# Projections, gated scan, silu and z in blocks of three chunks instead of segments of two, each in a PSUM bank of its own, with a new instruction list

**Chip, cores, metric.** One core of one Trainium2 chip. Times are device microseconds (us) of one execution; "span" is the time from the first to the last instruction of the profiled execution, which is 1.7 us or so shorter. Engines: TensorE (PE, its weight loads PEld), VectorE (DVE), ScalarE (ACT), GpSimd (POOL), SyncE (SP). The "granted clock" is the share of full speed that TensorE's clock was given. Every instruction is issued from one helper, so all have one line (L98, L99 or L100) in the profiles. Lower is better.

## The reference, cut to what matters

```python
# attention: B=4, H=8, S=768, D=48
for t in range(S):
    cur = einsum('bhd,bhe->bhde', u * k[t], v[t])
    y[t] = einsum('bhd,bhde->bhe', r[t], state + cur)
    state = w[t][..., None] * state + einsum('bhd,bhe->bhde', k[t], v[t])
x = y, heads side by side                     # (4, 768, 384)
proj = x @ w_in                               # 384 -> 2 * 512: val, gate
h = exp(A_log) * h + val[t]   for every t     # the gated scan over the sequence
out = (silu(gate) * h) @ w_out                # 512 -> 384
```

## The kernel before: the parts that the change and the argument touch

The sequence of 4 x 768 is cut into 24 chunks of 128 steps. A chunk of attention goes through all engines: products r\*P, k\*N (`Q`, `K`), transposes, scores (`sc`), the masked scores (`At`), the state (`S`), the output (`y`), and its transpose `xT`. The second half of the kernel works on segments of two chunks:

```python
SEG = 2 * C                                    # C = 128
xTs = ring("xT", 2, [128, 3, S_], BF16)        # two whole batches
hTs = ring("hT", 2, [128, NG, S_], BF16)
zs  = ring("z", 3, [128, NG, SEG], BF16)       # NG = 4 groups of 128 channels
att = psum.tile([C, 2, HP, C], F32)            # one tile of scores, no second one
mms = [psum.tile([128, 512], F32, name=f"mm{i}") for i in range(3)]

def project(m, g0, at):                        # two groups in one bank
    ps = mms[at].rearrange("p (j t) -> p j t", j=2)
    for j in range(2):
        for kk in range(3):
            pe.matmul(ps[:, j, :], w_in_sb[:, kk, (g0+j)*128:(g0+j+1)*128],
                      T["xT", b][:, kk, s*SEG:(s+1)*SEG], start=(kk==0), stop=(kk==2))
    return ps

def scn(m, gg):                                # VectorE, 256 steps
    dve.tensor_tensor_scan(hT[:, gg, s*SEG:(s+1)*SEG], a_f[...], T["pv", m, gg//2][:, gg%2, :],
                           0.0 if s == 0 else hT[:, gg, s*SEG-1:s*SEG], MUL, ADD)

def sl(m, q):                                  # ScalarE, 2 x 256 elements
    lut("silu", T["z", m][:, 2*q:2*q+2, :], T["pg", m, q], Silu)

def z(m, *, on):                               # VectorE ("d") or GpSimd ("p"), 4 x 256 elements
    MULT[on](T["z", m], T["z", m], T["hT", b][:, :, s*SEG:(s+1)*SEG])

def rk(m):                                     # both inputs in SBUF, always VectorE
    dve.tensor_mul(T["rk", m], T["rk", m], T["k", m])

def At(n):                                     # one input in PSUM (att), frees att for the next sc
    dve.tensor_mul(At_n, T["sc", n], mask)
```

The order of all instructions is a list of words in the program, one word an operation: `z.2:d` is the product z of segment 2 on VectorE, `K.5:p` the k\*N product of segment 5 on GpSimd. Each engine runs its own words strictly in the order of the list (in the timeline of VectorE below, the starts at 100.08, 102.01, 103.51, 105.59 and 106.05 us are the words `z.2.0`, `rk.9`, `z.2.1`, `y.15` and `At.17` of the changed list); semaphores do the rest. A cut of it:

```
... At.10 sl.0.0 cs.7.P:20 lw.4 sl.1.1 z.2:d out.9 ex.7.P.0 yT.8 z.1:d pv.3.1:1 lw.5
z.0:d adv.9 red.5 K.6:p xT.8 ld.9.w ex.7.P.1 tr.11 y.9 ...
```

## Time and profile before

| | before |
|---|---|
| time, median of 3 runs | 150.94 us (149.77 to 150.99) |
| profiled run | 149.59 us, span 147.9, mean granted TensorE clock 0.976 |
| VectorE busy | 123.4 us of the span |
| GpSimd busy | 93.7 us |
| start of y of chunks 8, 13, 18, 23 | 65.07, 92.41, 117.61, 135.70 us |

Read the table from its last row: y of a chunk is the last VectorE step of its attention, so the y starts are a clock of how far the kernel has got. They divide the span in a front (to y of 8), a middle (to y of 23), and a tail. In the middle VectorE is almost never idle (busy 69.63 of 70.63 us).

### The profile page before, as it was taken

How to read it: one execution, taken by the hardware profiler on the slowest of the kernel's cores; microseconds unless marked ns; L12 is line 12 of the kernel's file. 1: busy time of each engine (PE TensorE's matmuls, PEld its weight loads, DVE VectorE, ACT ScalarE, POOL GpSimd, SP SyncE). 2: the span in 40 equal slices, each digit the busy share in tenths (PEclk: the TensorE clock that was granted, in tenths of full speed). 3: DMA queues.
4: the chain of work that ended last, by engine and by line, in shares of the span. 5: the costliest groups of instructions: out<-in, count | busy, mean ns of one | idle time of the engine just before them, and what ended most of it. 6: DMA issues, size and time to landing. Idle time of an engine off the chain costs nothing.

```text
span 147.9 us, 3833 instructions
## 1 busy us (share of the span) xinstructions
PE 119.2 (81%) x1512; PEld 83.1 (56%) x1512; DVE 123.4 (83%) x169; ACT 99.0 (67%) x181; POOL 93.7 (63%) x83
## 2 busy tenths in 40 slices
PE   0286873899698778996199989998798899999990
PEld 0133541585475555775085667876576576777750
DVE  3027997577985799999999999989999999999750
ACT  3285626876746597999177979989677635664561
POOL 7806243194797969649490499999252897928500
PEclk9999999999999999999757999999999999999999
DMA  3999998999999899999999999975998996530435
GB/s 55 236 190 234 195 207 180 239 202 213 231 195 234 160 250 221 196 195 317 149 207 192 168 218 225 145 213 83 180 242 171 218 287 184 144 111 0 160 118 205
DMA packets 101026, 27.98 MB, mean 189 GB/s; under 512 B 95760, under 2 KB 101008, under 8 KB 101008
## 3 DMA queue, kind: packets, MB, share of 16 engines
q1 hardware_dynamic: 101008, 27.73, 94.7%
q8 instruction: 12, 0.20, 0.6%
q14 instruction: 6, 0.05, 0.1%
HBM read 21.43 MB, written 4.72 MB: 177 GB/s over the span
## 4 chain that ended last, share of the span: by engine, by line
DVE 44%; PE 27%; SPq 11%; DMA 6%; issue 6%; ACT 4%; DVEq 0%; ACTq 0%
PE mm L100 15%; DVE hT L100 12%; SPq L100 11%; DVE At L100 8%; DVE rk L100 8%; PE trp L100 5%; PE yk L100 5%; DVE y L100 5%; DVE z L100 4%; DMA w<-in_w_dram 4%; DVE dvec L100 3%; DMA k<-in_k_dram 2%; PE att L100 2%; DVE S L100 2%; ACT QK L100 1%
## 5 line engine op out<-in xcount | busy, mean ns | idle before, releaser
L100 PE MATMUL mm<-xT,w_in_sb 128*128 128x256 bf16 x288 | 39.6, 282 | 0.8 <-ACT xT L100 0.6
L100 PEld LDWEIGHTS <-w_in_sb 128*128 128x128 bf16 x288 | 27.3, 100 | 6.7 <-issue 1.8
L100 POOL TENSOR_TENSOR qk<-k,N 128x768 bf16<-128x768 f32 x11 | 21.8, 1981 | 14.3 <-DMA k<-in_k_dram 14.3
L100 DVE TENSOR_TENSOR At<-att,mask 128x1024 bf16<-128x1024 f32 x24 | 29.0, 1210 | 1.2 <-PE att L100 1.1
L100 POOL TENSOR_TENSOR qk<-r,P 128x768 bf16<-128x768 f32 x10 | 19.6, 1959 | 7.6 <-DMA r<-in_r_dram 7.4
L100 DVE TENSOR_TENSOR_SCAN hT<-a_f,hT,mm 128x256 bf16<-128x256 f32 x32 | 22.3, 730 | 1.3 <-PE mm L100 1.3
L100 POOL TENSOR_TENSOR dv<-v,dvec 128x768 f32<-128x768 f32 x9 | 13.3, 1473 | 14.6 <-DVE dvec L100 11.6
L100 ACT COPY QK<-trp 128x1024 bf16<-128x1024 bf16 x18 | 18.2, 1014 | 5.9 <-PE trp L100 5.7
L100 PEld LDWEIGHTS <-qk 128*48 128x48 bf16 (+1 forms) x304 | 16.0, 114 | 10.8 <-issue 7.6
L100 POOL TENSOR_TENSOR rk<-r,u_b 128x768 f32<-128x768 f32 x9 | 16.7, 1861 | 4.5 <-DMA u_b<-in_u_dram 4.5
L100 PEld LDWEIGHTS <-QK 48*128 48x128 bf16 x352 | 11.4, 103 | 13.4 <-ACT QK L100 5.9
L100 PE MATMUL mm<-w_out_sb,z 128*128 128x384 bf16 x96 | 18.9, 331 | 0.0
L100 DVE TENSOR_TENSOR rk<-rk,k 128x768 f32<-128x768 f32 x12 | 17.6, 1469 | 0.0
L100 ACT COPY osb<-mm 128x384 f32<-128x384 f32 x24 | 11.4, 479 | 8.1 <-PE mm L100 7.7
L100 ACT ACTIVATE z<-mm 128x512 bf16<-128x512 f32 x24 | 13.9, 599 | 3.8 <-PE mm L100 3.5
L100 PE MATMUL trp<-ident,qk 128*128 128x128 bf16 x144 | 15.3, 269 | 1.2 <-ACT xT L100 0.9
L100 ACT COPY xT<-trp 128x384 bf16<-128x384 bf16 x24 | 11.5, 481 | 6.7 <-PE trp L100 6.3
L100 DVE TENSOR_TENSOR y<-yk,dv 128x384 bf16<-128x384 f32 x24 | 13.1, 544 | 3.5 <-PE yk L100 3.4
L100 ACT ACTIVATE N<-mm 128x384 f32<-128x384 f32 x24 | 10.9, 489 | 7.6 <-PE mm L100 7.5
L100 PE MATMUL att<-QK 48*128 48x128 bf16 x192 | 11.2, 247 | 4.6 <-ACT QK L100 3.7
L100 ACT ACTIVATE P<-mm 128x384 f32<-128x384 f32 x24 | 10.8, 494 | 5.0 <-PE mm L100 5.0
L100 ACT ACTIVATE lwp<-w 128x768 bf16<-128x768 f32 (+1 forms) x13 | 10.2, 795 | 6.1 <-DMA w<-in_w_dram 5.9
(52 smaller groups left out, 182.0 us busy)
## 6 DMA issues: line engine op xcount, KB each, us to landing
k<-in_k_dram SPq DMA_DIRECT2D x24, 192.0 KB, 4.6
r<-in_r_dram SPq DMA_DIRECT2D x24, 192.0 KB, 4.8
v<-in_v_dram SPq DMA_DIRECT2D x24, 192.0 KB, 4.7
out_dram<-osb SPq DMA_DIRECT2D x24, 192.0 KB, 2.4
w<-in_w_dram SPq DMA_DIRECT2D x11, 384.0 KB, 5.4
stage<-in_moe_w_in_dram SPq DMA_DIRECT2D x4, 384.0 KB, 4.9
stage<-in_moe_w_out_dram SPq DMA_DIRECT2D x2, 384.0 KB, 4.6
w<-in_w_dram SPq DMA_DIRECT2D x2, 192.0 KB, 3.4
```

The costliest lines, as they stand in the source:

```text
L100: return lambda *args, **kwargs: self.tc.keep_in_program_order(op(*args, **kwargs))
```

## The change

The intent is fewer fixed costs: 384 steps at a time instead of 256 make 32 scans instead of 48 and 192 projection matmuls instead of 288, and a bank that holds one group is free again after one scan. z is cut in halves so that it can be spread over two engines. The list was worked out anew.

```diff
-    xTs = ring("xT", 2, [128, 3, S_], BF16)
-    hTs = ring("hT", 2, [128, NG, S_], BF16)
-    zs = ring("z", 3, [128, NG, SEG], BF16)
+    xTs = ring("xT", 3, [128, 3, BL], BF16)        # BL = 3 * C
+    hTs = ring("hT", 3, [128, NG, BL], BF16)
+    zs = ring("z", 3, [128, NG, BL], BF16)
...
-    def project(m, g0, at):
-        ps = mms[at].rearrange("p (j t) -> p j t", j=2)
-        for j in range(2):
-            for kk in range(3): ...
+    def project(mb, gg, at):
+        ps = mms[at][:, :BL]
+        for kk in range(3):
+            pe.matmul(
+                ps, w_in_sb[:, kk, gg * 128 : (gg + 1) * 128], T["xT", mb][:, kk, :],
+                start=(kk == 0), stop=(kk == 2))
...
+    def scn(mb, gg):
         dve.tensor_tensor_scan(
+            hT[:, gg, :], a_f[:, gg : gg + 1].to_broadcast([128, BL]), T["pv", mb, gg],
+            T["hT", mb - 1][:, gg, BL - 1 : BL] if mb * BL % S_ else 0.0, MUL, ADD)
...
-        MULT[on](T["z", m], T["z", m], T["hT", b][:, :, s * SEG : (s + 1) * SEG])
+        rows = slice(2 * q, 2 * q + 2)
+        MULT[on](T["z", mb][:, rows, :], T["z", mb][:, rows, :], T["hT", mb][:, rows, :])
... (the whole list is new; the place that the result turns on:)
+ sc.17 z.2.0:d sl.2.3 tr.16 ld.10.r.0 rk.9 sl.2.2 out.15 QK.16 pg.3.0:1 z.2.1:d ld.10.k.0
+ pg.4.2:2 y.15 dv.8:p sl.3.0 pg.3.3:0 At.17 sl.4.2 ld.11.w pv.4.0:1 sl.3.3 pg.4.0:2 vc.8:a K.9:p
+ scn.4.0 sc.16 pg.4.3:0 ship.1 sl.4.0 At.16 ... trd.18 out.16 ru.10:p S.17:d ...
```

In the list the words r\*P on VectorE go from 3 to 6, k\*N on VectorE from 2 to 4, r\*u on VectorE from 3 to 4, dv on VectorE from 3 to 2. (A word may be half a product.)

## The prediction

> **What bounds the kernel now.** I read the page's shares first, then busy time by stage, then the chain that ended last, the groups, and last the VectorE (DVE) and SyncE timelines. The shares show no single bound:
>
> ```profile
> PE 119.2 (81%) x1512; PEld 83.1 (56%) x1512; DVE 123.4 (83%) x169; ACT 99.0 (67%) x181; POOL 93.7 (63%) x83
> ...
> DVE 44%; PE 27%; SPq 11%; DMA 6%; issue 6%; ACT 4%; DVEq 0%; ACTq 0%
> ```
>
> VectorE has the most work and the largest part of the chain. The stage table (busy us of PE, PEld, DVE, ACT, POOL with counts, then granted clock, DMA share, GB/s) separates four regimes:
>
> ```profile
> 0.00:9.20 9.20, 2.15 (x13) 0.81 (x14) 1.43 (x10) 4.19 (x9) 6.06 (x33) 1.00 0.92 153
> 9.20:24.00 14.80, 10.51 (x117) 6.22 (x115) 12.73 (x16) 8.07 (x17) 5.11 (x3) 1.00 1.18 202
> 24.00:52.00 28.00, 24.05 (x304) 16.27 (x304) 20.63 (x29) 18.29 (x35) 20.20 (x12) 1.00 1.10 211
> 52.00:65.00 13.00, 11.18 (x159) 8.66 (x155) 12.97 (x16) 12.00 (x21) 8.65 (x5) 1.00 1.12 217
> 65.00:136.00 71.00, 63.08 (x873) 45.70 (x871) 70.00 (x93) 51.03 (x94) 51.24 (x29) 0.95 0.91 184
> 136.00:147.90 11.90, 8.26 (x60) 5.43 (x57) 5.61 (x9) 5.37 (x11) 2.39 (x2) 0.98 0.42 150
> ```
>
> To 9.2 the kernel waits for its first inputs. From 9.2 to 52 VectorE idles 9.4 us, in hand-overs and waits for loads. From 52 to 136 it is busy 83.0 of 84.0 us: it is the bound, and what it gains or loses there moves the end one for one. From 136 TensorE streams the last projections and outputs without a gap and VectorE has time to spare. The rows behind this:
>
> ```profile
> L100 DVE TENSOR_TENSOR At<-att,mask 128x1024 bf16<-128x1024 f32 x24 | 29.0, 1210 | 1.2 <-PE att L100 1.1
> L100 DVE TENSOR_TENSOR_SCAN hT<-a_f,hT,mm 128x256 bf16<-128x256 f32 x32 | 22.3, 730 | 1.3 <-PE mm L100 1.3
> L100 DVE TENSOR_TENSOR rk<-rk,k 128x768 f32<-128x768 f32 x12 | 17.6, 1469 | 0.0
> L100 DVE TENSOR_TENSOR_SCAN hT<-a_f,mm 128x256 bf16<-128x256 f32 x16 | 10.3, 670 | 0.0
> L100 DVE TENSOR_TENSOR z<-z,hT 128x1024 bf16<-128x1024 bf16 x7 | 9.1, 1332 | 0.1
> L100 POOL TENSOR_TENSOR qk<-r,P 128x768 bf16<-128x768 f32 x10 | 19.6, 1959 | 7.6 <-DMA r<-in_r_dram 7.4
> ```
>
> The rk product has minimum 927 ns and mean 1469; z has minimum 679 and mean 1332. That stretching is about 12 us in all (12 x 0.54 for rk, 7 x 0.65 for z, 1.25 for one r*u product). It falls on products with both inputs in SBUF, while GpSimd (POOL) runs one too:
>
> ```profile
> 75.59 2.06 POOL L100 TENSOR_TENSOR qk<-k,N 128x768 bf16<-128x768 f32 x1
> 75.90 2.56 DVE L100 TENSOR_TENSOR rk<-rk,k 128x768 f32<-128x768 f32 x1
> ```
>
> [...] Here 24 projections of 256 columns start in 2.86 us (119 ns each) and 24 output matmuls of 384 in about 4.0 us (167 each)[...].
>
> **The change, part by part.** I use spacing of back-to-back instructions of the VectorE timeline, which is some 70 to 90 ns less than a printed duration, since they overlap: At 1.13 us, y 0.46, S 0.26, rk and dvec 0.86, a scan 0.66 (0.60 where it starts from zero), a 768-wide product 0.87, z 0.62.
>
> 1. *Scans.* 48 of 256 become 32 of 384: equal elements, 16 fixed costs fewer. 32 x 0.66 + 16 x 0.60 = 30.7 us[...]. Saves 2.0 us of VectorE.
> 2. *Projections.* 288 matmuls of 256 columns become 192 of 384: 73,728 columns either way. 48 groups at 0.66 us against 64 at 0.5: 31.7 and 32. TensorE gains nothing but 96 weight loads of 100 ns, which mostly lie beside matmuls. A bank now holds one scan, not two, and comes free sooner after its three matmuls.
> 3. *Silu.* 24 of 512 elements (599 ns; spacing 0.49) become 32 of 384 (0.385, from 0.82 ns an element between the 384- and 512-wide rows): 11.8 to 12.3 us on ScalarE. Switches between exponential and silu tables, counted in both lists, stay at six loads. Nothing on the path.
> 4. *z.* Halves of 768 elements, 10 on VectorE and 6 on GpSimd, for 7 and 5 of 1024: VectorE 10 x 0.487 = 4.9 against 4.3; GpSimd 9.6 against 10.7.
> 5. *Work moved by the new list.* Counted from the lists, VectorE takes three more whole r*P products, two more whole k*N and one more r*u, and gives one dv away: 6 x 0.87 - 0.87 = +4.35 us. GpSimd loses about 9 us by that, some 10 with z.
> 6. VectorE in all, uncontended and without start-up: -2.0 + 0.6 + 4.35 = +2.9 us (108.2 to 111.0 as I sum all words).
>
> Where this falls matters. I summed the work listed ahead of each chunk's y. Up to y of chunk 8 (65.1 us before) both lists give VectorE 41.8 us, GpSimd 30.8 before and 19.0 after, TensorE 36.2 and 33.0, loads 13.2 and 12.4 MB. Most of the moved products are thus in the stage where VectorE idles, and replace a GpSimd product of 1.8 us by one of 0.95 within a dependent loop. From y of 8 to y of 23 VectorE has 61.1 before and 63.3 after. After y of 23 TensorE has 7.4 us before and 8.8 after: the last block is three chunks, so eight groups of projections (4.0 us) follow the last y instead of four (2.6).
>
> **Sum.** Front: idle is some 10 us ahead of 65, and I judge that 3 to 6 go: -4.5. Middle: +2.2 of work, plus contention. Fourteen products with two SBUF inputs lost about 0.55 us each there; the new list has 20, less a little for shorter GpSimd z: +1.5 to 3, taken as +2. Lost bubbles: TensorE once waited 4.1 us for a bank under two scans, and its clock fell to 0.55 and 0.60 in the next eight us (72 to 80); if that does not return, up to -2, taken as -1. I walked the last block by hand: y, 0.33 transposes, 0.48 copy, then eight projections, four scans of 0.93 in turn and seven outputs end about 10.1 us after y of 23, where before it was 8.65: +1.5. Together -4.5 + 2.2 + 2 - 1 + 1.5 = +0.2 us: no gain I can derive. A list that was worked out anew was presumably chosen because its whole schedule came out shorter, which I cannot see in sums; for this I take off 1.5 us.
>
> **Rivals.**
> *A, the schedule is the gain.* The loop in the front tightens fully and start-up idle falls by 8 us: 143 to 147. For: GpSimd falls from 30.8 to 19.0 us by y of 8, single-scan banks, fewer bytes wanted early. Against: TensorE itself is busy 24.05 of 28 us at 24 to 52, so there is little room.
> *B, VectorE becomes a harder bound.* The extra products are stretched as rk is today (1469 against 927), and the longer tail is paid in full: 152 to 155. For: 83.0 of 84.0 us busy. Against: GpSimd is 10 us emptier over the whole run.
> *C, supply sets the pace.* SyncE issues loads from 0.8 to 95 us almost without a gap, and the DMA share is about 1.1 to 65 us:
>
> ```profile
> q1 hardware_dynamic: 101008, 27.73, 94.7%
> ...
> POOL qk L100 <- DMA k<-in_k_dram: 14.3, 6, 4.2
> ```
>
> The change moves the same bytes in as many transfers, so whatever the engines gain ends in waits for k, r or v, and the time stays at 149 to 151. Against: later, SyncE waits 14.0 us for finished outputs, so supply is not short there.
>
> **Range and chances.** The before is 150.94 us by median, 149.59 in the profiled run with a span of 147.9. With -1.3 us net I predict 149.5 us. Front (3 us either way), contention (2), tail (1), and run differences (1) give about 3.9 in quadrature; I take 145.5 to 153.5. Faster by over 2% means below 147.9 (0.30); slower means over 153.96 (0.15); the rest, 0.55, is within.
>
> **What would show each step.** Right: 32 scans near 0.94 and 1.00 us; 192 projections of 384 columns and an unchanged busy TensorE within 3 us; VectorE busy 124 to 128 us, GpSimd 81 to 86; y of chunk 8 at 59 to 63 us; last y to end 13 to 13.5 us against 11.65; six table loads. Wrong: [...]VectorE below 122 us (contention fell with GpSimd's load, and I had the sign wrong); y of chunk 8 no earlier than 65 (supply bound, rival C); a new wait of several us of VectorE in the middle, where I assume none; a tail no longer than before.

## The result, and the profile after

| | before | after |
|---|---|---|
| median | 150.49 us (149.77 to 150.99, 4 runs) | 155.32 us (154.75 to 155.92, 4 runs) |
| ratio of fast runs | | 1.0325 (95%: 1.0251 to 1.0399): slower |
| profiled run | 149.59, span 147.9, clock 0.976 | 155.84, span 154.1, clock 0.956 |
| front, to y of 8 | 65.07 | 60.22 (-4.85) |
| middle, y of 8 to y of 23 | 70.63 | 80.23 (+9.6) |
| tail, from y of 23 | 12.20 | 13.65 (+1.45) |

A ratio here is the mean time of one kernel's fast runs over that of the other's in the same rounds, so not quite the ratio of the medians that are quoted. Executions over 1.5% slower than the fastest of the same kernel are left out of the means. The change lost 3%; the prediction had 149.5 us, with 153.5 as its upper end.

The page of the changed kernel, its shares and the chain of waits that ended last:

```profile
PE 121.0 (78%) x1416; PEld 72.0 (47%) x1416; DVE 129.5 (84%) x161; ACT 100.3 (65%) x189; POOL 84.2 (55%) x79
...
DVE 37%; PE 32%; issue 10%; ACT 6%; DMA 6%; POOL 4%; SPq 3%; DVEq 0%; POOLq 0%; ACTq 0%
```

VectorE has 6.1 us more to do than before. Yet its part of the chain fell from 44 to 37%, and TensorE's grew, and so did "issue", the time in which the engine waited for nothing that the profile shows. The groups of instructions of the changed kernel (total us, then mean ns):

```profile
L99 PE MATMUL mm<-xT,w_in_sb 128*128 128x384 bf16 x192 | 40.8, 346 | 2.0 <-DVE hT L99 1.8
L99 DVE TENSOR_TENSOR_SCAN hT<-a_f,hT,mm 128x384 bf16<-128x384 f32 x16 | 16.0, 1005 | 1.1 <-PE mm L99 0.8
L99 DVE TENSOR_TENSOR rk<-rk,k 128x768 f32<-128x768 f32 x12 | 15.3, 1274 | 0.0
L99 DVE TENSOR_TENSOR_SCAN hT<-a_f,mm 128x384 bf16<-128x384 f32 x16 | 14.8, 939 | 1.0 <-PE mm L99 0.9
L99 DVE TENSOR_TENSOR z<-z,hT 128x768 bf16<-128x768 bf16 x10 | 13.8, 1394 | 0.1
```

The scans cost just what was expected of them (939 and 1005 ns, for 0.94 and 1.00 us). z did not: its ten halves take 1394 ns on the mean, where the shortest took 545 (of the wholes of 1024 elements before: 679), so 8.5 us of their 13.8 is time spent blocked.

"Blocked" and "stretched" stand for what the timelines of before and after show of VectorE's products with two SBUF inputs. Of those with 768 elements of f32 input, 29 began with no GpSimd instruction running, or with at most 0.12 us of one left, and took 0.93 to 0.96 us; 13 began with 0.3 us or more of one left and took 1.11 to 2.56 us; one began at the same time as one (86.46 us, after) and took 0.95. The masked scores, with one input in PSUM, took 1.19 to 1.23 us and the reductions to dvec, with one input, 0.92 to 0.95, beside GpSimd or not.

Busy time by stage, before (stretch, its length, busy us of PE, PEld, DVE, ACT, POOL with counts, granted clock, DMA share, GB/s):

```profile
0.00:65.07 65.07, 47.96 (x584) 31.96 (x584) 47.83 (x69) 42.63 (x78) 40.02 (x53) 1.00 1.10 202
65.07:135.70 70.63, 62.71 (x869) 45.44 (x869) 69.63 (x92) 50.84 (x93) 50.94 (x29) 0.95 0.92 185
135.70:147.90 12.20, 8.56 (x64) 5.69 (x61) 5.91 (x9) 5.50 (x11) 2.69 (x2) 0.98 0.41 146
```

The same three stages after, then four us of the middle at a time:

```profile
0.00:60.22 60.22, 41.61 (x522) 25.50 (x523) 46.97 (x65) 38.89 (x72) 28.32 (x47) 0.97 1.13 203
60.22:140.45 80.23, 69.41 (x839) 41.34 (x838) 75.72 (x90) 55.08 (x105) 51.02 (x29) 0.94 0.89 171
140.45:154.10 13.65, 9.96 (x59) 5.19 (x56) 6.85 (x9) 6.28 (x13) 4.87 (x3) 1.00 0.41 145
104.00:108.00 4.00, 0.81 (x12) 0.55 (x12) 4.00 (x4) 0.79 (x2) 3.33 (x2) 1.00 0.48 111
108.00:112.00 4.00, 4.00 (x46) 2.18 (x46) 2.41 (x4) 2.00 (x4) 0.00 (x0) 0.57 0.01 4
```

In the middle VectorE is busy 75.7 us instead of 69.6 (+6.1) and idle 4.5 us instead of 1.0 (+3.5); that is the +9.6. By place, 4.7 of it comes before y of 13, where the front's lead is used up (92.25 us, and 92.41 before), 5.2 between y of 13 and y of 18, and -0.3 after that. Of the +6.1, 3.3 is stretching: over the unblocked durations the products with two SBUF inputs lose 11.9 us there, and lost 8.6 before.

The two last rows show a hole. From 104 to 108 us TensorE works 0.81 us of four while VectorE is full; from 108 to 112 it is the other way about, the clock is at 0.57, and the DMA moves 4 GB/s. The timeline of VectorE in the changed kernel (start, length) tells what fills it:

```profile
98.94 1.21 DVE L99 TENSOR_TENSOR At<-att,mask 128x1024 bf16<-128x1024 f32 x1
100.08 2.01 DVE L99 TENSOR_TENSOR z<-z,hT 128x768 bf16<-128x768 bf16 x1
102.01 1.57 DVE L99 TENSOR_TENSOR rk<-rk,k 128x768 f32<-128x768 f32 x1
103.51 2.15 DVE L99 TENSOR_TENSOR z<-z,hT 128x768 bf16<-128x768 bf16 x1
105.59 0.54 DVE L99 TENSOR_TENSOR y<-yk,dv 128x384 bf16<-128x384 f32 x1
106.05 1.21 DVE L99 TENSOR_TENSOR At<-att,mask 128x1024 bf16<-128x1024 f32 x1
```

GpSimd in the same stretch:

```profile
99.86 1.82 POOL L99 TENSOR_TENSOR qk<-k,N 128x768 bf16<-128x768 f32 x1
...
102.74 2.51 POOL L99 TENSOR_TENSOR rk<-r,u_b 128x768 f32<-128x768 f32 x1
```

And TensorE, where the bracket is its idle time before the instruction and what ended it:

```profile
101.52 2.60 PE L99 MATMUL mm<-xT,w_in_sb 128*128 128x384 bf16 x15
107.31 0.40 PE L99 MATMUL att<-QK 48*128 48x128 bf16 x8 [3.19 <-DVE At L99]
```

Read the three together. The half products z of block 2 and the product rk of segment 9 stand in VectorE's list ahead of y of 15 and the masked scores of chunk 17. GpSimd's k\*N begins at 99.86 and its r\*u at 102.74, each ahead of a z. Without blocking z, rk, z would take 0.54 + 0.93 + 0.54 = 2.0 us; they take 5.7. TensorE runs out its projections at 104.1 and then cannot score chunk 16, because the one tile of scores is still waiting to be masked. It idles 3.19 us. From 108.2 us, 0.9 us after it has come back, its clock is halved for 3.4 us (0.50 over 108.2 to 111.6). SyncE has a transposing copy (`trd.19`) in its queue, whose buffer is that of chunk 16 and comes free with the output matmuls of chunk 16; it waits 7.2 us for them, to 111.4, with loads and stores queued behind it, so the DMA stops too.

Such a hole is nothing new. VectorE of the kernel before:

```profile
66.67 4.26 DVE L100 TENSOR_TENSOR z<-z,hT 128x1024 bf16<-128x1024 bf16 x3
```

and its TensorE:

```profile
73.48 0.82 PE L100 MATMUL mm<-lwp,triP 64*128 64x384 bf16 x4 [4.01 <-DVE hT L100]
```

Three z in a row took 4.26 us, and TensorE idled 4.0. The prediction saw that hole, and reckoned that the new list would be rid of it.

### The profile page after: what moved, and what is told of

Read it like the earlier page. It is cut to its first block, busy times and chain, and to the rows that moved or that the text cites.

```text
span 154.1 us, 3607 instructions
## 1 busy us (share of the span) xinstructions
PE 121.0 (78%) x1416; PEld 72.0 (47%) x1416; DVE 129.5 (84%) x161; ACT 100.3 (65%) x189; POOL 84.2 (55%) x79
## 4 chain that ended last, share of the span: by engine, by line
DVE 37%; PE 32%; issue 10%; ACT 6%; DMA 6%; POOL 4%; SPq 3%; DVEq 0%; POOLq 0%; ACTq 0%
PE mm L99 19%; DVE hT L99 10%; DVE At L99 7%; DVE z L99 6%; PE trp L99 6%; PE yk L99 5%; DVE y L99 4%; DVE qk L99 4%; DVE rk L99 3%; SPq L99 3%; DMA r<-in_r_dram 3%; DMA v<-in_v_dram 3%; PE att L99 2%; DVE S L99 2%; POOL qk L99 2%
## 5 line engine op out<-in xcount | busy, mean ns | idle before, releaser
L99 PE MATMUL mm<-xT,w_in_sb 128*128 128x384 bf16 x192 | 40.8, 346 | 2.0 <-DVE hT L99 1.8
L99 POOL TENSOR_TENSOR qk<-k,N 128x768 bf16<-128x768 f32 x9 | 17.6, 1952 | 18.2 <-ACT N L99 14.2
L99 PEld LDWEIGHTS <-w_in_sb 128*128 128x128 bf16 x192 | 17.9, 101 | 15.1 <-issue 6.0
L99 ACT ACTIVATE z<-mm 128x384 bf16<-128x384 f32 x32 | 15.2, 491 | 10.4 <-PE mm L99 10.1
L99 POOL TENSOR_TENSOR qk<-r,P 128x768 bf16<-128x768 f32 x7 | 14.9, 2129 | 10.9 <-ACT P L99 10.2
L99 PE MATMUL trp<-ident,qk 128*128 128x128 bf16 x144 | 14.8, 262 | 5.8 <-DVE qk L99 4.5
L99 DVE TENSOR_TENSOR_SCAN hT<-a_f,hT,mm 128x384 bf16<-128x384 f32 x16 | 16.0, 1005 | 1.1 <-PE mm L99 0.8
L99 DVE TENSOR_TENSOR_SCAN hT<-a_f,mm 128x384 bf16<-128x384 f32 x16 | 14.8, 939 | 1.0 <-PE mm L99 0.9
L99 DVE TENSOR_TENSOR rk<-rk,k 128x768 f32<-128x768 f32 x12 | 15.3, 1274 | 0.0
L99 DVE TENSOR_TENSOR y<-yk,dv 128x384 bf16<-128x384 f32 x24 | 13.1, 545 | 2.5 <-PE yk L99 2.3
L99 DVE TENSOR_TENSOR z<-z,hT 128x768 bf16<-128x768 bf16 x10 | 13.8, 1394 | 0.1
L99 PE MATMUL mm<-lwp,triN 64*128 64x384 bf16 (+1 forms) x46 | 8.0, 401 | 7.3 <-ACT lwp L99 5.7
```

What stands on the lines that cost most here:

```text
L99: return lambda *args, **kwargs: self.tc.keep_in_program_order(op(*args, **kwargs))
```

## The experiments

The theory after this reading, the **place theory**: the loss is where the blocked products stand, with the attention loop waiting right behind them, and is worth some 4 to 5 us. Rivals: the **amount theory**, that VectorE was simply given too many products with two SBUF inputs, wherever they stand; later the **supply theory**, that loads set the pace, and the **clock theory**, that the fall of TensorE's clock is the loss. Kernels of one group ran on the same chip. Every edit is to words of the list unless it says otherwise; results are right unless it says otherwise.

**1. The two z moved back behind the masked scores.**

```diff
- sc.17 z.2.0:d ... pg.3.0:1 z.2.1:d ... At.17 ... At.16 ... S.17:d yT.15
+ sc.17 ... pg.3.0:1 ... At.17 ... At.16 ... S.17:d z.2.0:d z.2.1:d yT.15
```

> The two halves of z of block 2 stay on VectorE but move in its list from before the mask products of chunks 17 and 16 to after the state product of chunk 17, where VectorE stood idle 1.5 us. Work per engine is unchanged. Amount theory (the middle is longer because VectorE has more work there): no change, 154.5 to 156. Place theory (the loss is made where stretched products stand ahead of a mask product for which TensorE waits, 3.2 us of TensorE idle and then a clock of 0.57): the products meet an idle GpSimd, 3 us of stretching and the idle go, 150.5 to 152.5. Supply theory (the late stages wait for loads): no change or under 1 us.

Median 150.95 us (150.32 to 152.96) beside 151.47 of before on that chip, ratio 0.998 (0.9918 to 1.0042): the same as before. Against the changed kernel's 155.32, measured in another round, that is 4.4 us from moving two words. VectorE in this kernel:

```profile
109.17 1.01 DVE L98 TENSOR_TENSOR z<-z,hT 128x768 bf16<-128x768 bf16 x2
```

Both halves now take 1.01 us together instead of 2.01 and 2.15, and the hole in TensorE is gone: from y of 14 to y of 18 it is 19.95 us instead of 24.45. That stretch in the changed kernel, and then here:

```profile
98.22:122.67 24.45, 19.17 (x223) 10.86 (x224) 22.83 (x26) 14.66 (x30) 13.11 (x8) 0.93 0.74 137
99.82:119.77 19.95, 17.64 (x223) 10.39 (x224) 19.54 (x25) 14.65 (x30) 12.49 (x8) 1.00 0.87 165
```

Of the 4.5 us, 3.3 are busy time of VectorE (22.83 to 19.54) and 1.2 its idle time (1.62 to 0.41). So this edit changes two things at once: where the z stand, and how long they last, 0.5 us each at the new place. The profiled run (152.96) is 1.6 us behind the changed kernel at y of 13 (93.83 us), so only this later stretch is compared.

**2. The two z on GpSimd, at their old place.**

```diff
- z.2.0:d ... z.2.1:d
+ z.2.0:p ... z.2.1:p
```

> The same two halves go to GpSimd at their old place. VectorE loses 4.2 us of measured time at 100 to 106 us. Amount theory: 151 to 152. Place theory: as the run before, 150.5 to 152.5, if GpSimd's later products (dv of 8, k*N of 9) are not wanted at once; it has 6 us idle at 107 to 113. If GpSimd now stands waiting for silu with the next products behind it: 155 to 158.

153.43 us (150.99 to 155.41), ratio 1.0158 (1.0085 to 1.0231), unclear by the 2% line. In the profiled run, which is the quickest (150.99), the hole is gone: y of 14 to y of 18 takes 21.18 us, and no wait of TensorE in the middle is over 1.6 us. The runs scatter over 4 us, so no more is drawn from it.

**3. Three of the added products given back to GpSimd, the two z left alone.**

```diff
- K.5:d (after Q.5 and ru.6)   Q.7:d   Q.8:d
+ K.5:p (right after Q.5)      Q.7:p   Q.8:p
```

> The three products that the new list moved to VectorE in the middle (k*N of 5, r*P of 7 and 8) go back to GpSimd, k*N of 5 right after r*P of 5. VectorE loses 2.6 us of bare work and 1.7 of stretching. Amount theory: 151 to 152. Place theory: only the first one stood before a wait of TensorE, so 153 to 154.5, and more stretching of what stays on VectorE.

155.78 us (155.12 to 156.31), ratio 1.0312 (1.026 to 1.0363): as slow as the changed kernel. VectorE is still busy 128.5 us: it has fewer products, but, with three more on GpSimd, its rk and z lose more (17.2 us of stretching instead of 15.8). The same hole stands there, from y of 14 at 97.44 to y of 15 at 104.81. **The amount theory falls here.** Taking three products away does nothing while the two z stay in their place, though VectorE's busy time fell by 1.0 us only; experiment 4 takes more.

**4. All z of blocks 0 to 6 on GpSimd.**

```diff
- z.0.0:d z.0.1:d z.1.0:d z.1.1:d z.2.0:d z.2.1:d z.3.0:d z.3.1:d z.5.1:d
+ z.0.0:p z.0.1:p z.1.0:p z.1.1:p z.2.0:p z.2.1:p z.3.0:p z.3.1:p z.5.1:p
```

> All z but those of the last block go to GpSimd at their places in the list: VectorE loses 9 products, 4.4 us bare and 8.5 of stretching; GpSimd gains 14.8 of 29 idle us in the middle. Amount theory: 146 to 149. Place theory: GpSimd now waits in order for scans and silu with the r and k products behind it, and rk meets a busier GpSimd: 151 to 158.

151.84 us (150.09 to 153.44), ratio 1.0014 (0.9937 to 1.0091): as good as experiment 1, with VectorE down to 123.2 us busy and GpSimd up to 99.9. 6.3 us less work on VectorE gives no more than moving two words, which again speaks for place and not for amount. What is left is two other waits of TensorE of 1.9 and 2.0 us, the first for a z that is now on GpSimd.

**5. More moves of the same kind, on top of experiment 1.**

```diff
- K.5:d (after Q.5)    z.0.1:d ... z.0.0:d (ahead of At.10)
+ K.5:p (after Q.5)    z.0.1:d z.0.0:d (after scn.2.3)
```

> On top of the first experiment, k*N of 5 goes to GpSimd right after r*P of 5 (on VectorE it took 2.6 us, blocked, with TensorE waiting 1.3 us for it), and the two z of block 0 move from before the mask product of chunk 10 to after the scans of block 2. Place theory: 2 to 3 us less than the first experiment's 150.95, so 148 to 149.5 and faster than the kernel before. Amount theory: at most the 0.9 us of one bare product, about 150. If the stretching only moves to other products: 150.5 to 152.

151.71 us (148.14 to 152.71), before 150.33 on that chip. **No gain over experiment 1, so what the place theory promised further did not come.** This trace has new waits instead: TensorE waits 1.86 us for a z at 75 and 1.3 us for a scan at 98.6.

On the chip of experiments 5 to 8 the runs of before lay at 149.66 to 151.9, but for one at 145.89, and the quickest run of a kernel makes the others count as slow; no ratio was formed there, and medians of all runs are compared.

**6 and 7. Delay alone.** On top of experiment 1, a sum over weights that nobody reads was put on VectorE at the two old places of z. It has one input, as the reductions to dvec have, which were not blocked in the traces of before and after (0.92 to 0.95 us, 11 of 24 beside GpSimd instructions). The fillers took 0.54 us (384 elements) and 2.12 us (1900), each pair alike. Only the length differs.

```diff
+ def dm(n): dve.reduce_sum(dummy, w_in_sb[:, :n], axis=AX)
- sc.17 ... pg.3.0:1 ... y.15 ... At.17
+ sc.17 dm.384 ... pg.3.0:1 dm.384 ... y.15 ... At.17      (experiment 6)
+ sc.17 dm.1900 ... pg.3.0:1 dm.1900 ... y.15 ... At.17    (experiment 7)
```

> The first experiment with two fillers on VectorE at the old places of the two z: reductions of 384 elements of one SBUF tensor, some 0.54 us each, as long as an unblocked z[...]. If the blocking (3.1 us on the two z) made the loss: 151 to 152, the first experiment plus about 1. If merely having two instructions there made it: 154 to 156.

152.13 us (150.22 to 153.37).

> The same with fillers of 1900 elements, about 2.1 us each, as long as the two z were when blocked (2.01 and 2.15). If time before the mask product is what costs, whatever fills it: 154.5 to 156.5, as the changed kernel. [...]

156.79 us (152.56 to 158.16); had the loss come from the blocking itself, and not from VectorE's delay, 151 to 153 was expected. Twice 1.58 us of filler, 3.2 us, cost 4.7. TensorE in the kernel with the long filler:

```profile
107.19 0.61 PE L98 MATMUL att<-QK 48*128 48x128 bf16 x8 [2.83 <-DVE At L98]
```

With the short filler that wait is 0.48 us, and the median is 1.2 us above that of experiment 1 (on another chip), about what two fillers last. **It is the length, 2.1 us each, that costs there.** Nothing but delay ahead of the masked scores is needed to make the hole. How much of the 4.7 us is due to the place is not shown: the long fillers are also 3.2 us more work for VectorE, and the same fillers at a place where nobody waits were not run. One of the four runs with the long filler was at 152.56, with a granted clock of 1.0; it makes the other three count as slow, so medians are compared here too.

**8. The same cure for the kernel before.** Its hole at 66.67 has the same shape, so its three z were moved back.

```diff
- z.2:d out.9 ... z.1:d ... z.0:d adv.9 ... S.10 ... scn.3.1 ... S.11
+ out.9 ... adv.9 ... S.10 z.0:d ... scn.3.1 z.1:d ... S.11 z.2:d
```

> The kernel before, with its three z in a row at 66.7 us (4.3 us, blocked; TensorE then waits 4.1 us for a scan and its clock falls) spread to later places: after the state product of 10, after the last scan of block 3, after the state product of 11. Place theory: 2 to 4 us faster than before, ratio 0.975 to 0.985. Amount theory: ratio 1.00. If the first result was luck of one list: 1.00 to 1.02.

149.72 us (148.99 to 151.55) beside 150.33. y of 9 comes 3.3 us earlier (68.41 instead of 71.71), and all of it is gone by y of 11 (85.38 and 85.53): an r\*u product of VectorE met GpSimd at 77.4 and took 2.57 us, and TensorE waited 2.34 us for masked scores. The hole formed anew one chunk on. As a recipe the place theory fails here too.

**9. The clock alone, in the changed kernel.** Twelve matmuls whose result nobody reads, ahead of the scores that the hole delays, keep TensorE from idling there but for 1.25 us.

```diff
- sc.16
+ wm.12:0 sc.16       # 12 x matmul(bank 0, ident, w_in_sb[:, 0, :384])
```

> The changed kernel as it is, with twelve useless matmuls of 384 columns (about 2 us) into a free bank just ahead of the scores of chunk 16, where TensorE idles 3.2 us. They fill the idle and add nothing else. If the fall of the clock after the idle (0.57 over 108 to 112 us, some 1.7 us of TensorE time) carries part of the loss: no fall there and 153 to 154 instead of 155.3. If only the idle itself counts: 155 to 156. If the matmuls delay the scores: 156 or more.

The windows of this kernel:

```profile
104.00:108.00 4.00, 2.75 (x23) 1.58 (x22) 4.00 (x5) 0.43 (x2) 2.71 (x2) 1.00 0.34 70
108.00:112.00 4.00, 3.69 (x68) 2.15 (x66) 3.63 (x6) 3.66 (x7) 0.60 (x1) 1.00 0.32 61
```

The clock now stays at 1.00 where it was 0.57, and TensorE does 68 matmuls in four us instead of 46. From y of 15 to y of 16 it is 6.01 us instead of 7.32, and from there to the end 41.2 us in both. The median is 155.28 us (153.91 to 156.66), no change against 155.32, but the runs scatter over 2.8 us, so it cannot show 1.3. See runs 14 and 15.

**10 and 11. Fewer loads.** The four loads of r and k of segment 6 are dropped, in the kernel of experiment 1 and in before; the products use stale data. Their outputs are wrong, which doesn't matter for the times.

```diff
- ld.6.r.1 ld.6.r.0 ld.6.k.1 ld.6.k.0
+ lx.6.r.1 lx.6.r.0 lx.6.k.1 lx.6.k.0     # names the buffer, loads nothing
```

> The first experiment without the four loads of r and k for half-pairs of block 6 (old values stay, so the result is wrong on purpose): 0.8 MB and some 4 us of the issuing queue less, and all later loads come that much sooner. Supply theory (the front gain of 5 us at chunk 8 is gone at chunk 13 because loads set the pace there): y of chunk 13 moves from 93.8 to 89 to 91, the whole to 146.5 to 149. If VectorE's work sets it: y of 13 stays within 1 us, 150 to 151.

154.41 us (154.07 to 154.96), where experiment 1 had 150.95 on another chip (with the upper runs of before at 150.6 to 151.0 here and 150.4 to 151.6 there); y of 13 at 95.14, later and not earlier than 93.83. The trace has other meetings instead: TensorE has waits of 2.86 us for a VectorE product at 68 and of 2.27 us for masked scores at 76.6, and rk loses 8.9 us to stretching.

> The kernel before without the same four loads (wrong on purpose). Supply theory: y of chunk 11 to 13 comes 2 to 4 us sooner than 85.5 and 92.4, the whole 2 to 4 us faster, ratio 0.973 to 0.987. Otherwise ratio 0.99 to 1.00.

150.53 us (147.84 to 152.09) beside 150.56; y of 13 at 94.28, in a profiled run of the slow state, after 92.41. **The supply theory falls in both kernels,** as far as these four loads go; no others were dropped. Why the first grew slower by as much as 3.5 us was not followed further than those lines.

**12. The front's products back on GpSimd, on top of experiment 1.**

```diff
- ru.2:d Q.2:d K.2:d
+ ru.2:p Q.2:p K.2:p
```

> The first experiment with the three early products that the new list moved to VectorE (r*P and k*N and r*u of 2) back on GpSimd. My front step: y of chunk 8 comes 1.5 to 4 us later than 59.3, and the end 1 to 3 us later, if nothing absorbs it. Supply theory: y of 8 later, but y of 13 within 1 us of 93.8 and the end unchanged (150 to 152).

150.76 us (150.25, 150.52, 151.01, and 154.34); y of 8 at 60.73 instead of 59.28, the end unchanged. So 1.4 us of the front's gain is not worth anything at the end. The profiled run is fast; its front, middle and tail are 60.73, 74.15 and 13.7 us, which is -4.3, +3.5 and +1.5 against before.

**13 to 16. Before and after once more, with and without useless matmuls, on one chip.** On the chip of runs 9 to 12 three of the seven runs of before lay at 146.0 to 146.2, the others at 150.6 to 151.0. The question was whether the clock makes these levels, and what it is worth.

```diff
13 (before):            + wm.18:2 ahead of cs.8.P (the wait of 4.0 us)
14 (after):             unchanged
15 (after):             + wm.14:0 ahead of sc.16
16 (experiment 1):      + wm.8:0 ahead of yT.11
```

> The kernel before with 18 useless matmuls (about 2.9 us) in the 4.0 us that TensorE idles at 69.4 us, in a bank that is free there. If the two levels of the kernel before (146.0 to 146.2 at a mean clock of 0.97 to 1.00, and 150.6 to 151.0 at 0.92 to 0.965) come from the clock's fall after this idle: nearly all runs at 146 to 147.5, ratio to the before of its median level 0.97. If the clock is only an accompaniment of a different course of the run: both levels stay, median 150 to 151.

149.43 us (148.81 to 150.13), six runs on one level, beside eleven runs of before: five at 144.4 to 145.4, six at 148.55 to 150.5. The clock of its profiled run (148.81) is 0.988, as high as in the lower runs of before (0.975 to 0.988), and still it is 3.4 us above the slowest of these: the upper level does not need a fallen clock. The other five runs had 0.942 to 0.965.

> The changed kernel again, on the chip of the others, as the base for the next run: 154.5 to 156.

155.2 us (153.99 to 157.47). The changed kernel repeats.

> The changed kernel with 14 useless matmuls ahead of the scores of chunk 16 (12 left 1.25 us idle and gained 1.9 us in the profiled run, but not by the median of four). If the clock after that idle carries 1.7 us of the loss: 153 to 154, 1.5 to 2 us below the changed kernel on this chip. Otherwise no difference over 0.5.

153.76 us (152.58 to 156.77). The fast runs have a mean of 153.57 against 154.80 of run 14, so 1.2 us; single runs differ by more. The traces agree: y of 15 to y of 16 takes 7.45 us in run 14 and 6.02 here, and the rest to the end 41.2 us in both. The clock theory is left with some 1.3 us of the five, within this one hole.

> The first experiment with 8 useless matmuls ahead of the transposes of y of chunk 11, where TensorE idled 1.9 us and its clock then fell (0.81 over 84 to 93 us). If the clock sets the level: 148.5 to 150, against 150.95. Otherwise 150.5 to 151.5.

152.0 us (151.38 to 153.93): no gain over experiment 1. The mean of its fast runs is 151.76, so on this chip the two moved words, with these matmuls, are worth 3.0 us against run 14, and not 4.4.

The ratios of runs 9 to 16 (1.0595, 1.057, 1.0186, 1.0305, 1.0323, 1.0688, 1.0603, 1.0478) are formed against the lower level of before, which those chips reached. Against before's six upper runs there (mean 149.8) the fast runs of 14 give 154.80 / 149.8 = 1.033, as in the first result. Which level one takes matters more than most edits here.

**17 and 18. The kernel before, unchanged, twice, each with a profile,** to catch the lower level in a trace.

> The kernel before, unchanged, for a trace of its lower level (144.4 to 146.2 us in 9 of 29 runs beside the experiments, none of them traced). If the lower level comes up: a trace in which one stage is 4 to 5 us shorter. Place theory: it is a stage where a stretched product or z stands ahead of what TensorE waits for (66 to 84 us, or 96 to 104). Clock theory: the same course with a clock of 1.0 throughout.

> The same once more, for a second draw between the two levels; expectations as for the first.

151.4 us (span 149.6) and 147.32 us (span 145.5), the same program; the second is 1.1 us above the slowest lower run seen so far. VectorE in the second:

```profile
59.62 0.95 DVE L100 TENSOR_TENSOR rk<-rk,k 128x768 f32<-128x768 f32 x1
...
63.21 1.88 DVE L100 TENSOR_TENSOR z<-z,hT 128x1024 bf16<-128x1024 bf16 x3
```

and its GpSimd:

```profile
61.30 1.81 POOL L100 TENSOR_TENSOR qk<-r,P 128x768 bf16<-128x768 f32 x1 [1.82 <-DMA r<-in_r_dram]
65.32 1.82 POOL L100 TENSOR_TENSOR qk<-k,N 128x768 bf16<-128x768 f32 x1 [2.21 <-DMA k<-in_k_dram]
```

The three z that took 4.26 us take 1.88: GpSimd waits for a load from 63.11 to 65.32 and blocks nothing. The load is no earlier or later than in the first profile of before, where the same product of GpSimd starts at 65.11; what differs is VectorE, which comes to its z at 63.21 us instead of 66.67. Its lead over that profile is 1.4 us at y of 7 and 3.5 at y of 8, after an rk of 0.95 us instead of 2.30, and 5.8 at y of 9 (65.88 and 71.71). By y of 13 it is down to 2.1 us, and at y of 23 it is 2.4 (133.34 and 135.70). So the same program does meet GpSimd's products in one execution and not in another, but most of what the three z saved is lost again.

The other run of the pair, 17, is behind by 3.9 us at y of 8, that is ahead of the z, and there the clock differs. The stretch from 36 to 57 us in run 17, then in run 18:

```profile
36.00:57.00 21.00, 17.00 (x192) 10.54 (x194) 15.08 (x21) 11.81 (x22) 17.36 (x12) 0.59 1.02 224
36.00:57.00 21.00, 16.59 (x241) 11.32 (x242) 18.12 (x27) 15.29 (x29) 17.23 (x12) 0.92 1.03 225
```

In the first profile of before the clock is 1.00 there. So neither reading explains the levels: blocked products and a clock that fell in the front both occur, and what decides between the levels stays open.

## Why the prediction was wrong, point by point

The sum of the prediction and what the traces gave for each term, in us:

| term | predicted | measured |
|---|---|---|
| front, to y of 8 | -4.5 | -4.85 |
| middle, bare VectorE work | +2.2 | +2.8 (6.1 busy less 3.3 stretching) |
| middle, contention | +2 | +3.3 |
| middle, lost bubbles | -1 | +3.5 (VectorE idle) |
| tail | +1.5 | +1.45 |
| sum | +0.2 | +6.2 (span 147.9 to 154.1) |
| "presumably chosen because its whole schedule came out shorter" | -1.5 | nothing of the kind |

- *Scans, projections, tables: right.* 32 scans of 0.94 and 1.00 us, TensorE busy within 1.8 us, GpSimd 84.2 us, six table loads. Larger blocks do save fixed costs; they are small: all scans together take 30.8 us (16.0 and 14.8) instead of 32.6 (22.3 and 10.3), so 1.8 us, where the estimate was 2.0.
- *Front and tail: right, to 0.4 us.* y of 8 came at 60.2, within 59 to 63. VectorE's idle time up to there fell from 17.2 to 13.2 us, within the 3 to 6 that the prediction judged would go; experiment 12 gives 1.4 us to three moved products, and the rest was not taken apart. From the end of the last y to the end of the span it is 13.1 us, within 13 to 13.5.
- *Contention: the stretching is there, mis-sized.* VectorE is busy 129.5 us, above the 124 to 128. The extra stretching is 3.3 us in the middle, not 2 (the prediction took 0.55 us for each of 14 products there; the trace of before has 8.6 us on 13, or 0.66 each). The two z of block 2 alone lose 3.1 us, and the stretching moved from rk (mean 1469 to 1274 ns) to z (545 at its shortest, 1394 on the mean).
- *The step that failed: "Lost bubbles ... if that does not return, up to -2, taken as -1".* It looked at the one bubble of the list before and asked if it would go. It did not ask where the new list would put its own. VectorE's idle time in the middle rose by 3.5 us where 1 us was taken off: the longest wait, 1.50 us, is in the new hole, and six of 0.2 to 0.8 us make up the rest. The hole itself counts in two rows of the table, as stretching and as idle time: moving its two z (experiment 1) took 3.3 us of busy and 1.2 us of idle time off the stretch, 4.4 us off the median. That this is near the 4.5 us between -1 and +3.5 is chance. A walk of VectorE's new list with blocked durations, z at some 2 us and rk at 1.5, could have found z, rk, z ahead of the masked scores of 17 and 16. I walked the last block by hand but summed the middle.
- *The 1.5 us taken off on top* had no line of a profile behind it, and put the number on the wrong side of the sum.
- *Rival B* had the right size (152 to 155; the median is just above) for half the right reason. VectorE's stretching is there, but giving work back to GpSimd (experiment 3) does not help. Rival A's front is there and is lost behind it; rival C falls by experiments 10 and 11, as far as they go. The prediction's last list did name "a new wait of several us of VectorE in the middle, where I assume none". What came is seven such waits, 4.4 us in all, and one wait of 3.19 us of TensorE.

With the hole out of the way (experiment 1) the change comes to 0.998 of before (0.9918 to 1.0042), which agrees with the +0.2 us of the derived sum within the noise. The fast profile of experiment 12, the same kernel but for three front products, has -4.3, +3.5 and +1.5 us in front, middle and tail, where the sum has -4.5, +3.2 and +1.5. The gain is then where the sum had put it, in the front, and is paid out again in the middle and the tail.

**What stays open.** What uses up the front's lead between y of 8 and y of 13; the loads of segment 6 do not (experiments 10 and 11). What makes the two levels of before. Whether a blocked z costs anything where no engine waits behind it, since the moved z were no longer blocked. And what a schedule must be like to keep blocked products away from waiting loops altogether: experiments 5, 8, 10 and 16 each made the holes move, not go. No version here beat the kernel before: the quickest by median, run 13 (149.43) and experiment 8 (149.72), are within its scatter, and before's own lower level is at 145.

## What to carry to other kernels

Sum the work, but then walk the new order of the busiest engine with the durations that blocked instructions really have, and look at what waits right behind each: two products of 0.5 us became 2 us each and cost 4.4 us in one place, and later in the list they kept their 0.5 us and cost nothing that shows. Products with two SBUF inputs on VectorE were safest here where they began with no GpSimd instruction running (0.93 to 0.96 us for 768 elements of f32, and up to 2.56 otherwise) and no other engine waited for the next VectorE instruction; experiments 5 and 8, which moved others by this rule, gained nothing, so it is an aim and not a recipe. And a kernel may have levels, as this one has about 145 and 150 us, for a reason that stays open: run it often, on more than one chip, before a difference of 3% is believed, and don't pay for a schedule's good intentions.

## What the traces show of single costs

- A blocked product: a half z, of 768 elements, takes 545 ns at its shortest, and 2.01 and 2.15 us beside GpSimd products (at 100.08 and 103.51 us of the changed kernel). What such a block is worth to a whole kernel: here two blocked z lost 3.1 us themselves and cost 4.4 us, while TensorE stood waiting behind them.
- Spacing of matmuls: those of 384 columns are 162 ns apart in a steady run (15 in 2.60 us against 6 in 1.14, in the changed kernel).
- TensorE's clock: in the changed kernel it is 0.50 from 108.2 to 111.6 us, and the 3.4 us before that hold 0.9 us of matmuls (the wait was 3.19 us, from 104.1 to 107.3). It is 0.50 from 67.3 us too, where the longest wait just before was 1.5 us. What makes it fall is not shown.
- The scan's fixed cost: about 132 ns, an estimate from two widths (670 ns at 256 elements and 939 at 384 give 2.10 ns an element). With a starting value that is read from SBUF a scan takes 60 to 66 ns more (730 and 1005).
